# Attention steps of a three-stage kernel: chunk 3 of the scores behind the values, the slot sums behind the reciprocals of head 1, and one copy of x on ScalarE

## The chip, the cores and the metric

The kernel runs on one core of a Trainium2 chip. The metric is the device time of one execution in microseconds; the kernel before was run three times, and its median stands for it. One execution was also profiled, which gives the trace of every engine.

## What is computed

Causal attention over 4 batches, 12 heads, 448 positions and 64 dimensions per head; its output, 1792 tokens of 768, goes through a soft mixture of experts (8 experts with 4 slots each, a softmax over tokens into the slots and one over slots back to the tokens) and then through a feed-forward layer with the activation h cos h.

```python
scores = scale * np.matmul(q, k.transpose(0, 1, 3, 2))      # causal mask, softmax
attn_out = np.matmul(attn, v)                               # per batch and head
x = attn_out.transpose(0, 2, 1, 3).reshape(B * S, H * D)

logits = x @ phi                                            # 1792 x 32
d = softmax(logits, over tokens);  slot_input = d.T @ x
slot_out[e] = np.maximum(slot_input[e] @ w1[e], 0.0) @ w2[e]
x = softmax(logits, over slots) @ slot_out

h = x @ w_in
out = (h * np.cos(h)) @ w_out
```

## The kernel before

Everything is one program for one core, in fp32. The change touches the attention alone, which fills some 225 us of the span; the expert weights stream in behind it, and the feed-forward layer follows.

Heads are handled in pairs: 4 batches with 6 pairs each, 24 pairs in all. Each pair's scores are cut into four chunks of query rows, `qk_mm(p, c)`: chunks 0, 1 and 2 hold 128 queries against 448, 320 and 192 keys, chunk 3 the last 64 queries of both heads against 64 keys. The two heads are j = 0 and 1. Each of the eight PSUM banks is named: banks 0 and 1 take chunk 0 of the two heads, and bank 0 also takes chunk 3 in its last 64 columns (line 281); banks 2 and 3 take chunks 1 and 2. `TA` and `TB` are banks 4 and 5, `OB` bank 6, `MB` bank 7.

For each pair the work goes through these helpers:

- `score` on VectorE adds the mask, takes the row minimum of the negated scores and writes them to SBUF (lines 308 and 311). It returns the exponential on ScalarE (line 313), which also sums the rows.
- `recip` on VectorE inverts the sums of one head (lines 320 and 321), and `norm` on GpSimd scales the exponentials (line 330), four instructions for head 0 (with chunk 3) and three for head 1.
- `t_pair` transposes one half of the normalised scores on TensorE in 64-column blocks into `TA` and `TB` (line 333). `ev_t` copies the two banks to SBUF, one by ScalarE (line 179) and one by VectorE (line 181).
- `pv` multiplies by the values on TensorE into `OB` (line 377), and `ev_o` copies the result by ScalarE into `xts` (line 179), which is x transposed.
- `x_t` transposes x back on TensorE (line 389), head 0 into `OB` and head 1 into bank 1, and `ev_x` copies both into `xk` (line 181), 112 partitions with 256 columns each.

Once per batch comes the part of the experts that needs attention's output: `phi_round` (line 400) gives the logits in `MB`, `be_logits` copies them, `be_rep` (line 409) spreads them, `be_d` takes maximum and exponential, `be_tok` (line 434) and `be_dk` (line 429) transpose them, and `be_u` (line 456) sums x into the slots, one half of a batch's pairs at a time. Its result is added to `uacc` by VectorE (line 460 in the first batch, line 462 later).

The order is written out by hand: `pair_step(t)` issues work of three pairs, `t` (scores), `p1 = t - 1` (normalising and transposing) and `p2 = t - 2` (values and x), and each engine runs its instructions in the order in which they are written there. So an instruction that waits holds up all that stands behind it on its engine. `pair_step` is called for t from 0 to 24; then `tail` closes the last pair and batch. `sc` and `e` call `score` and the exponential that it returned.

Of the kernel before, what the change touches and what calls it, by code (L numbers as in the profile page):

```python
# [15 lines left out]
NB, NH, S, D = 4, 12, 448, 64  # L16
# [140 lines left out]
def moe_stack_kernel(ctx: ExitStack, tc: tile.TileContext, qk, v, cst, phi, w1, w2, w_in, w_out, out):  # L157
    nc = tc.nc

    def pr(key):  # L160
        def deco(fn):
            def run(*a):
                k = key(*a) if callable(key) else key
                if callable(key) and k not in PRI and "." in k:
                    k = k[:k.index(".")]
                o = PRI.get(k, 0)
                if not o:
                    return fn(*a)
                with tc.high_priority(o):
                    return fn(*a)  # L170
            return run
        return deco
# [4 lines left out]
    def copy(e, o, i):  # L177
        if e == "A":
            ACT.activation(o, i, AF.Copy)
        else:  # L180
            ENG[e].tensor_copy(o, i)  # L181
# [85 lines left out]
    def V(p, c, j):  # L267
        c0, n, t = [x for x in VB[p % 2] if x[0] <= c < x[0] + x[1]][0]
        o = 128 * (c - c0) + 64 * j
        return t[:, o:o + 64]  # L270

    def XT(p):
        return xts[:, (p % 4) * 448:(p % 4 + 1) * 448]

    def XK(p):
        i = p % 7
        return xks[i // 4][0:112, (i % 4) * 512:(i % 4 + 1) * 512].rearrange("p (r f) -> p r f", r=4)
# [6 lines left out]
    @pr(lambda p, c: f"qk{c}")  # L284
    def qk_mm(p, c):
        if c == 3:

            for j in range(2):
                PE.matmul(bank[0][64 * j:64 * j + 64, 448:512], lhsT=Q(p)[:, 384 + 64 * j:448 + 64 * j],
                          rhs=K(p)[:, 0:64], start=True, stop=True)  # L290
            return
        q0, ln = CH[c]
        for j in range(2):
            h = slice(64 * j, 64 * j + 64)
            PE.matmul(sreg(j, c), lhsT=Q(p)[h, q0:q0 + 128], rhs=K(p)[h, 0:ln], start=True, stop=True)  # L295

    @pr(lambda p, j, c: f"score{j}{c}")
    def score(p, j, c):
        st_ = pst[p % 2]
        if c == 3:  # L300
            dst, ln, m, col = P0(p), 64, mask0, 3
        else:
            ln = CH[c][1]
            dst, m, col = Pt(p, j)[:, PO[c]:PO[c] + ln], (mask, mask[:, 128:], mask2)[c], 4 * j + c
        sb = sreg(j, c)
        if c == 2:
            blk = lambda x: x.rearrange("p (b f) -> p b f", f=64)
            DVE.tensor_tensor_reduce(out=blk(dst), in0=blk(sb), in1=m, scale=-0.125, scalar=3.0e38,
                                     op0=ALU.add, op1=ALU.min, accum_out=st_[:, col:col + 1])
        else:  # L310
            DVE.tensor_tensor_reduce(out=dst, in0=sb, in1=m, scale=-0.125, scalar=3.0e38,  # L311
                                     op0=ALU.add, op1=ALU.min, accum_out=st_[:, col:col + 1])
        return pr(f"exp{j}{c}")(lambda: ACT.activation(dst, dst, AF.Exp, bias=st_[:, col:col + 1], scale=-1.0,  # L313
                                                       accum_out=st_[:, 8 + col:9 + col]))
# [52 lines left out]
    @pr("pv")  # L367
    def pv(p):
        pt = [pts[:, 1024 * j:1024 * j + 1024] for j in range(2)]
        ops = [(384, 448, 0, [pt[0][:, 384:448], pt[0][:, 960:1024]], True, True),  # L370
               (0, 384, 0, [t[:, 0:384] for t in pt], True, False),
               (64, 384, 1, [t[:, 448:768] for t in pt], False, False),
               (128, 320, 2, [t[:, 768:960] for t in pt], False, False),
               (256, 320, 3, [pt[1][:, 384:448]] * 2, False, True)]
        for a, b, c, r, first, last in ops:
            for j in range(2):
                PE.matmul(OB[64 * j:64 * j + 64, a:b], lhsT=V(p, c, j), rhs=r[j], start=first, stop=last)  # L377

    @pr("evo")
    def ev_o(p):  # L380
        copy(CFG["evo"], XT(p), OB[:, 0:448])
# [3 lines left out]
    @pr("xt")  # L385
    def x_t(p):
        for r in range(4):
            for j, h in enumerate((LO, HI)):
                PE.transpose(XB[j][0:112, 64 * r:64 * r + 64], XT(p)[h, 112 * r:112 * r + 112],
                             cs[h, 64:128] if j else cs[h, 0:64])  # L390

    @pr("evx")
    def ev_x(p, j, e):
        copy(e, XK(p)[:, :, 64 * j:64 * j + 64], XB[j][0:112, 0:256].rearrange("p (r f) -> p r f", r=4))

    @pr("phi")
    def phi_round(b, pr):
        for i in pr:
            r = i % 4
            PE.matmul(MB[32 * r:32 * r + 32, 0:448], lhsT=phs[:, i, :], rhs=XT(b * NPB + i),  # L400
                      start=(i < 4), stop=(i + 4 >= NPB))

    @pr("logits")
    def be_logits(b):
        ACT.activation(ltr, MB[:, 0:448], AF.Copy)
# [26 lines left out]
    def be_tok(b):  # L432
        for r in range(4):
            PE.matmul(MB[0:112, 128 + 32 * r:160 + 32 * r], lhsT=ltr[:, 112 * r:112 * r + 112], rhs=rep[:, 0:32],
                      start=True, stop=True)
        DVE.tensor_copy(ctok[:, 4 * b:4 * b + 4, :], MB[0:112, 128:256].rearrange("p (r s) -> p r s", r=4))
# [14 lines left out]
    def be_u(b, half):  # L451
        ub = TB if (b, half) == (NB - 1, 1) else MB
        for i in range(3):
            p = b * NPB + 3 * half + i
            for r in range(4):
                PE.matmul(ub[32 * r:32 * r + 32, 128 * i:128 * i + 128], lhsT=dk[0:112, r, :], rhs=XK(p)[:, r, :],
                          start=True, stop=True)
        u = uacc[:, 384 * half:384 * half + 384]
        if b == 0:
            DVE.tensor_copy(u, ub[:, 0:384])  # L460
        else:
            DVE.scalar_tensor_tensor(u, u, st[:, 9:10], ub[:, 0:384], op0=ALU.mult, op1=ALU.add)


    def keep_warm(n, t=cs):
        for _ in range(n):
            PE.matmul(bank[3 if t is cs else 7][:, 0:128], lhsT=t[:, 0:128], rhs=t[:, 0:128], start=True, stop=True)
# [14 lines left out]
    def sc(t, j, c):  # L482
        if t < NPAIR:
            ex[j, c] = score(t, j, c)

    def e(t, j, c):
        if t < NPAIR:
            ex[j, c]()

    def pair_step(t):  # L490

        now, prv, pr2 = t < NPAIR, 0 <= t - 1 < NPAIR, 0 <= t - 2 < NPAIR
        bo = {t - NPB * b: b for b in range(NB)}
        p1, p2 = t - 1, t - 2
        if now:
            qk_mm(t, 0)
        if t == 0:
            keep_warm(6, uacc)
        if prv:
            sc(p1, 1, 1)  # L500
            e(p1, 1, 1)
            sc(p1, 1, 2)
            e(p1, 1, 2)
        if 6 in bo:
            phi_round(bo[6], range(4))
        if 8 in bo:
            phi_round(bo[8], range(4, NPB))
            be_logits(bo[8])
        if 9 in bo:
            be_tok(bo[9])  # L510
            be_dk(bo[9])
        sc(t, 0, 0)
        e(t, 0, 0)
        sc(t, 1, 0)
        e(t, 1, 0)
        if now:
            qk_mm(t, 3)
        if pr2:
            pv(p2)
        if 9 in bo:  # L520
            be_u(bo[9], 0)
        if 10 in bo:
            be_u(bo[10], 1)
        if 8 in bo:
            be_rep(bo[8])
        if prv:
            recip(p1, 1)
            for c in range(3):
                norm(p1, 1, c)
        sc(t, 0, 3)  # L530
        if pr2:
            ev_o(p2)
        if prv:
            t_pair(p1, 0)
            ev_t(0, "A")
            ev_t(1, "D")
        e(t, 0, 3)
        if now:
            qk_mm(t, 1)
            qk_mm(t, 2)  # L540
        if 8 in bo:
            be_d(bo[8])
        sc(t, 0, 1)
        e(t, 0, 1)
        sc(t, 0, 2)
        e(t, 0, 2)
        if pr2:
            x_t(p2)
            ev_x(p2, 1, "D")
            ev_x(p2, 0, "D")  # L550
        if prv:
            t_pair(p1, 1)
            ev_t(2, "A")
            ev_t(3, "D")
        if now:
            recip(t, 0)
            for c in range(4):
                norm(t, 0, c)
        if t < NPAIR - 2:
            load_raw(t + 2)  # L560
        if 1 < t < NPAIR:
            load_v(t)
        if t >= 1 and t % 6 != 0 and len(pieces) < NPRE:
            load_piece()
        for _ in range(PL.get(t, 0)):
            load_piece()
# [577 lines left out]
```

## Time and profile before

| what | value |
|---|---|
| median of three runs | 579.81 us (579.77 to 582.02) |
| the profiled execution | 578.87 us, its span 577.1 us |
| TensorE matmul busy, share of the span | 512.5 us, 89% |
| TensorE weight load | 365.2 us, 63% |
| VectorE | 355.1 us, 62% |
| ScalarE | 309.5 us, 54% |
| GpSimd | 184.1 us, 32% |
| DMA moved | 100.36 MB, mean 174 GB/s |
| mean granted TensorE clock | 0.964 of full speed |

The span is from the first to the last instruction; the time of the execution holds some 1.8 us around it. Busy shares are means over stages with different limits: the attention runs to about 225 us, then the expert weights are streamed (to about 300 us), then the feed-forward layer keeps TensorE at 90% and more. Where engines wait is told by the waits and by the timeline of a step, which the prediction goes through.

### The profile page before, as it was taken

What the parts mean: (1) busy time and instruction counts of PE and PEld (TensorE: products, weight loads), DVE (VectorE), ACT (ScalarE), POOL (GpSimd) and SP (SyncE); (2) the same over time, 40 slices, a digit from 0 to 9 for tenths busy, and PEclk for the clock granted to TensorE, in tenths of its full rate; (3) what the DMA queues carried; (4) which work ended last, traced back from release to release, by engine and by line L of the source; (5) the groups of instructions that cost most, each with busy time, mean ns of one, the idle gap of its engine ahead of it and who ended that gap; (6) DMA issues with size and microseconds to landing.
All of it is one profiled execution on the core that took longest, in us unless ns stands there. A gap on an engine that the chain in (4) does not pass through costs nothing.

```text
span 577.1 us, 11159 instructions
## 1 busy us (share of the span) xinstructions
PE 512.5 (89%) x4292; PEld 365.2 (63%) x4292; DVE 355.1 (62%) x897; ACT 309.5 (54%) x711; POOL 184.1 (32%) x251
## 2 busy tenths in 40 slices
PE   6889877887888888988868899999999999999997
PEld 4555545544555556332446687778787777888997
DVE  4575656764774564610148889988798887534532
ACT  3676756764675461101128676665656746543552
POOL 1344424432442340000004352424344246522231
PEclk9798989987997889999999999999999999999999
DMA  5476546573655458999993425332325301202201
GB/s 177 147 250 219 177 142 235 179 247 99 215 165 210 154 213 298 378 422 421 419 367 118 170 82 188 109 110 73 146 84 191 109 1 56 109 1 109 111 1 55
DMA packets 24245, 100.36 MB, mean 174 GB/s; under 512 B 2816, under 2 KB 6912, under 8 KB 18048
## 3 DMA queue, kind: packets, MB, share of 16 engines
q1 hardware_dynamic: 24192, 99.66, 47.8%
q8 instruction: 33, 0.54, 0.4%
q14 instruction: 20, 0.16, 0.1%
HBM read 94.14 MB, written 5.51 MB: 173 GB/s over the span
## 4 chain that ended last, share of the span: by engine, by line
PE 50%; DVE 21%; DMA 15%; ACT 7%; issue 3%; POOL 3%; SPq 0%; DVEq 0%; ACTq 0%; POOLq 0%
PE bank L377 9%; PE bank L879 7%; PE bank L877 7%; PE bank L878 7%; PE bank L295 7%; DMA w<-in_w_dram 6%; DMA zraw<-in_w_out_dram 5%; PE bank L333 5%; DMA zraw<-in_w_in_dram 4%; DVE p L311 3%; POOL p L330 2%; DVE zscr L858 2%; ACT zraw L703 2%; DVE zscr L864 2%; ACT zscr L861 2%
## 5 line engine op out<-in xcount | busy, mean ns | idle before, releaser
L877 PE MATMUL bank<-zg,zhl 128*128 128x512 f32 (+1 forms) x378 | 140.0, 370 | 0.3 <-ACT zhl L725 0.3
L878 PE MATMUL bank<-zg,zhl 128*128 128x512 f32 (+1 forms) x378 | 137.7, 364 | 0.9 <-DVE zhl L738 0.9
L879 PE MATMUL bank<-zg,zhl 128*128 128x512 f32 (+1 forms) x378 | 137.5, 364 | 0.8 <-POOL zg L870 0.8
L870 POOL TENSOR_TENSOR zg<-zscr,zg 128x512 fp32r<-128x512 f32 (+1 forms) x64 | 82.8, 1298 | 140.3 <-ACT zg L867 120.2
L330 POOL TENSOR_SCALAR p<-p,pst 128x448 f32<-128x448 f32 (+3 forms) x168 | 81.3, 502 | 134.8 <-DVE pst L321 94.8
L313 ACT ACTIVATE p<-p,pst 128x448 f32<-128x448 f32 (+3 forms) x168 | 87.5, 521 | 41.6 <-DVE pst L311 41.6
L877 PEld LDWEIGHTS bank<-zg,zhl 128*128 128x128 f32 x378 | 71.5, 189 | 13.7 <-issue 1.4
L878 PEld LDWEIGHTS bank<-zg,zhl 128*128 128x128 f32 x378 | 71.6, 189 | 12.3 <-DVE zhl L738 1.6
L879 PEld LDWEIGHTS bank<-zg,zhl 128*128 128x128 f32 x378 | 71.4, 189 | 12.5 <-POOL zg L870 1.3
L295 PE MATMUL bank<-qk 64*128 64x192 f32 (+2 forms) x288 | 63.0, 466 | 3.5 <-DVE xk L181 3.5
L858 DVE SCALAR_TENSOR_TENSOR zscr<-zscr,bank 128x512 f32<-128x512 int32 (+1 forms) x64 | 38.8, 618 | 32.8 <-ACT zscr L855 32.5
L861 ACT ACTIVATE zscr<-zscr,b_h 128x512 f32<-128x512 f32 (+1 forms) x64 | 42.0, 669 | 31.5 <-DVE zscr L858 31.4
L181 DVE COPY pts<-bank 128x512 f32<-128x512 f32 x48 | 33.0, 687 | 41.8 <-PE bank L333 41.8
L311 DVE CUSTOM_DVE_ANT_0 p<-bank,cs 128x448 f32<-128x448 f32 (+1 forms) x96 | 50.7, 547 | 9.7 <-PE bank L295 9.7
L864 DVE TENSOR_TENSOR zscr<-bank,zscr 128x512 f32<-128x512 f32 (+1 forms) x64 | 39.1, 621 | 18.4 <-ACT zscr L861 18.4
L855 ACT ACTIVATE zscr<-bank,b_q 128x512 int32<-128x512 f32 (+1 forms) x64 | 39.4, 629 | 20.2 <-PE bank L851 20.1
L867 ACT ACTIVATE zg<-zscr 128x512 fp32r<-128x512 f32 (+1 forms) x64 | 36.2, 575 | 26.0 <-DVE zscr L864 25.9
L738 POOL TENSOR_TENSOR zhl<-uacc,zhl 128x768 fp32r<-128x768 f32 (+1 forms) x7 | 10.8, 1550 | 101.6 <-ACT zhl L725 101.6
L703 ACT ACTIVATE zraw<-zraw 128x768 f32<-128x768 f32 x32 | 29.2, 911 | 24.6 <-DMA zraw<-in_w_in_dram 13.2
L333 PE MATMUL bank<-cs,p 64*128 64x64 f32 (+1 forms) x768 | 35.2, 230 | 6.8 <-POOL p L330 6.6
L295 PEld LDWEIGHTS bank<-qk 64*128 64x128 f32 x288 | 29.3, 194 | 14.1 <-DVE xk L181 9.9
L333 PEld LDWEIGHTS bank<-cs,p 64*128 64x128 f32 (+1 forms) x768 | 29.1, 137 | 12.5 <-POOL p L330 10.1
(142 smaller groups left out, 703.7 us busy)
## 6 DMA issues: line engine op xcount, KB each, us to landing
w<-in_w_dram SPq DMA_DIRECT2D x48, 1024.0 KB, 7.9
zraw<-in_w_in_dram SPq DMA_DIRECT2D x16, 768.0 KB, 4.4
zraw<-in_w_out_dram SPq DMA_DIRECT2D x16, 768.0 KB, 4.3
qk<-in_qk_dram SPq DMA_DIRECT2D x24, 480.0 KB, 3.6
xk<-in_v_dram SPq DMA_DIRECT2D x12, 256.0 KB, 3.9
out_dram<-zps SPq DMA_DIRECT2D x8, 256.0 KB, 2.0
xts<-in_v_dram SPq DMA_DIRECT2D x12, 128.0 KB, 3.5
lt<-in_v_dram SPq DMA_DIRECT2D x12, 128.0 KB, 4.1
```

Source lines behind the costliest of these rows:

```text
L295: PE.matmul(sreg(j, c), lhsT=Q(p)[h, q0:q0 + 128], rhs=K(p)[h, 0:ln], start=True, stop=True)
L311: DVE.tensor_tensor_reduce(out=dst, in0=sb, in1=m, scale=-0.125, scalar=3.0e38, op0=ALU.add, op1=ALU.min, accum_out=st_[:, col:col + 1])
L313: return pr(f"exp{j}{c}")(lambda: ACT.activation(dst, dst, AF.Exp, bias=st_[:, col:col + 1], scale=-1.0, accum_out=st_[:, 8 + col:9 + col]))
L330: ENG[CFG["norm"][3 * j + c if c < 3 else 6]].tensor_scalar(dst, dst, st_[:, 24 + col:25 + col], 0.0, op0=ALU.mult, op1=ALU.add)
L333: PE.transpose(out, src, by)
L377: PE.matmul(OB[64 * j:64 * j + 64, a:b], lhsT=V(p, c, j), rhs=r[j], start=first, stop=last)
L861: ACT.activation(y_(s), y_(s), AF.Sin, bias=b_h, scale=1.0)
L864: DVE.tensor_tensor(y_(s), hb[:, 0:n_(s)], y_(s), ALU.mult)
L870: eng.tensor_tensor(g_(s)[1], y_(s), g_(s)[0].bitcast(F32), ALU.subtract)
L877: PE.matmul(o, lhsT=wh, rhs=gh, start=first, stop=False)
L878: PE.matmul(o, lhsT=wl, rhs=gh, start=False, stop=False)
L879: PE.matmul(o, lhsT=wh, rhs=gl, start=False, stop=last)
```

## The change

Three moves inside `pair_step`. The two matmuls of chunk 3 are issued behind `pv` instead of ahead of it. The two calls of `be_u` stand behind `sc(t, 0, 3)` and `ev_o` instead of ahead of `recip(p1, 1)`. `x_t` and the copy of head 1's half of x stand ahead of the exponential of chunk 1, and that copy is made by ScalarE ("A") instead of VectorE ("D"); the copy of head 0's half stays where it was, on VectorE.

```diff
--- before.py
+++ after.py
@@ -513,14 +513,10 @@
         e(t, 0, 0)
         sc(t, 1, 0)
         e(t, 1, 0)
+        if pr2:
+            pv(p2)
         if now:
             qk_mm(t, 3)
-        if pr2:
-            pv(p2)
-        if 9 in bo:
-            be_u(bo[9], 0)
-        if 10 in bo:
-            be_u(bo[10], 1)
         if 8 in bo:
             be_rep(bo[8])
         if prv:
@@ -530,6 +526,10 @@
         sc(t, 0, 3)
         if pr2:
             ev_o(p2)
+        if 9 in bo:
+            be_u(bo[9], 0)
+        if 10 in bo:
+            be_u(bo[10], 1)
         if prv:
             t_pair(p1, 0)
             ev_t(0, "A")
@@ -541,12 +541,13 @@
         if 8 in bo:
             be_d(bo[8])
         sc(t, 0, 1)
+        if pr2:
+            x_t(p2)
+            ev_x(p2, 1, "A")
         e(t, 0, 1)
         sc(t, 0, 2)
         e(t, 0, 2)
         if pr2:
-            x_t(p2)
-            ev_x(p2, 1, "D")
             ev_x(p2, 0, "D")
         if prv:
             t_pair(p1, 1)
```

TensorE, at the start of step 12 (a step with four rounds of `phi_round`). bank_64 is bank 0, bank_65 bank 1, bank_70 `OB`, bank_71 `MB`, bank_68 and bank_69 `TA` and `TB`. Before:

```order
L295 MATMUL bank_64<-qk 128x448
L295 MATMUL bank_65<-qk 128x448
L400 MATMUL bank_71<-xts,phs 32x448 x4
L289 MATMUL bank_64<-qk 64x64 x2
L377 MATMUL bank_70<-pts,xk_77 64x64 x2
L377 MATMUL bank_70<-pts,xk_77 64x384 x2
L377 MATMUL bank_70<-pts,xk_77 64x320 x2
L377 MATMUL bank_70<-pts,xk_77 64x192 x2
L377 MATMUL bank_70<-pts,xk_77 64x64 x2
L333 MATMUL bank_68<-cs,p_74 128x64
```

In the change:

```order
L295 MATMUL bank_64<-qk 128x448
L295 MATMUL bank_65<-qk 128x448
L400 MATMUL bank_71<-xts,phs 32x448 x4
L377 MATMUL bank_70<-pts,xk_77 64x64 x2
L377 MATMUL bank_70<-pts,xk_77 64x384 x2
L377 MATMUL bank_70<-pts,xk_77 64x320 x2
L377 MATMUL bank_70<-pts,xk_77 64x192 x2
L377 MATMUL bank_70<-pts,xk_77 64x64 x2
L289 MATMUL bank_64<-qk 64x64 x2
L333 MATMUL bank_68<-cs,p_74 128x64
```

Chunk 3 (line 289) went from ahead of the ten matmuls of `pv` (two instructions each in the trace) to behind them; the transposes of half 0 (line 333) follow it.

VectorE, in the first step with a `be_u` (step 9); line 460 is its slot sum, lines 320 and 321 are the reciprocals of head 1 and the line 311 behind them is the score of chunk 3:

```order
 L311 ISA p_74,pst_88<-bank_65,cs 128x448
 L311 ISA pst_88 128x1
+L320 TENSOR_SCALAR pst_87<-pst_87 128x3
+L321 RECIPROCAL pst_87<-pst_87 128x3
+L311 ISA p_74,pst_88<-bank_64,qk 128x64
+L311 ISA pst_88 128x1
 L460 COPY uacc<-bank_71 128x384
-L320 TENSOR_SCALAR pst_87<-pst_87 128x3
-L321 RECIPROCAL pst_87<-pst_87 128x3
-L311 ISA p_74,pst_88<-bank_64,qk 128x64
-L311 ISA pst_88 128x1
```

The reciprocals and the score of chunk 3 went ahead of the slot sum.

ScalarE, in an early ordinary step, from the copy of `TA` to the next one. Before:

```order
L179 ACTIVATE pts<-bank_68 128x8x64
L313 ACTIVATE p_73,pst_87<-p_73,pst_87 128x64
L313 ACTIVATE p_73,pst_87<-p_73,pst_87 128x320
L313 ACTIVATE p_73,pst_87<-p_73,pst_87 128x192
L179 ACTIVATE pts<-bank_68 128x8x64
```

In the change:

```order
L179 ACTIVATE pts<-bank_68 128x8x64
L313 ACTIVATE p_73,pst_87<-p_73,pst_87 128x64
L179 ACTIVATE xk_77<-bank_65 112x4x64
L313 ACTIVATE p_73,pst_87<-p_73,pst_87 128x320
L313 ACTIVATE p_73,pst_87<-p_73,pst_87 128x192
L179 ACTIVATE pts<-bank_68 128x8x64
```

The copy of head 1's half of x (out of bank 1) now stands between the exponentials of chunk 3 and of chunk 1.

## Rows read from the trace of the kernel before

**Rows 1.** Busy time by step: window, its length, engines busy us (count), PEclk, DMA share, GB/s.

```profile
29.47:36.73 7.26, 5.85 (x77) 3.88 (x77) 5.11 (x23) 5.43 (x18) 3.38 (x8) 1.00 0.68 238
...
67.37:78.40 11.03, 8.72 (x90) 5.44 (x90) 6.43 (x28) 6.85 (x23) 4.15 (x10) 1.00 0.72 261
...
88.52:96.99 8.47, 6.21 (x100) 4.24 (x101) 5.63 (x24) 5.55 (x18) 3.38 (x8) 1.00 0.63 229
...
131.88:142.71 10.83, 8.49 (x100) 5.50 (x101) 5.64 (x24) 5.39 (x16) 2.62 (x5) 0.78 0.25 79
...
sum 184.80, PE 151.99 PEld 96.39 DVE 114.76 ACT 119.01 POOL 71.08; mean PE 7.24 PEld 4.59 DVE 5.46 ACT 5.67 POOL 3.38
```

**Rows 2.** Who waited for whom, TensorE, 20 to 215: us total, times, longest.

```profile
PE bank L289 <- DVE pst L311: 24.5, 22, 1.9
```

**Rows 3.** Timeline of TensorE in one step: start, us, line, shapes, count, [idle before].

```profile
151.26 0.34 PE L289 MATMUL bank<-qk 128*64 128x64 f32 x4 [1.36 <-DVE pst L311]
151.42 1.47 PE L377 MATMUL bank<-pts,xts 128*64 128x64 f32 x12
...
153.26 0.71 PE L333 MATMUL bank<-cs,p 64*128 64x64 f32 x16
153.81 1.08 PE L295 MATMUL bank<-qk 64*128 64x320 f32 x8
154.73 0.39 PE L389 MATMUL bank<-cs,xts 64*112 64x64 f32 x8
154.95 0.71 PE L333 MATMUL bank<-cs,p 64*128 64x64 f32 x16
155.50 1.61 PE L295 MATMUL bank<-qk 64*128 64x448 f32 x4
157.04 0.96 PE L400 MATMUL bank<-xts,phs 128*32 128x448 f32 x8
158.52 0.34 PE L289 MATMUL bank<-qk 128*64 128x64 f32 x4 [0.52 <-DVE pst L311]
```

**Rows 4.** Timeline of VectorE in the same step.

```profile
151.66 0.17 DVE L320 TENSOR_SCALAR pst<-pst 128x3 f32<-128x3 f32 x1
...
154.04 0.69 DVE L181 COPY pts<-bank 128x512 f32<-128x512 f32 x1 [1.89 <-PE bank L333]
...
155.62 0.75 DVE L181 COPY xk<-bank 112x256 f32<-112x256 f32 x2
...
156.89 0.16 DVE L320 TENSOR_SCALAR pst<-pst 128x4 f32<-128x4 f32 x1
...
157.18 0.46 DVE L311 CUSTOM_DVE_ANT_0 p<-bank,cs 128x320 f32<-128x320 f32 x1
...
157.84 0.62 DVE L311 CUSTOM_DVE_ANT_0 p<-bank,cs 128x448 f32<-128x448 f32 x1
```

**Rows 5.** Timeline of ScalarE in the same step.

```profile
153.38 0.55 ACT L179 ACTIVATE xts<-bank 128x448 f32<-128x448 f32 x1 [0.57 <-PE bank L377]
154.07 0.60 ACT L179 ACTIVATE pts<-bank 128x512 f32<-128x512 f32 x1
154.56 0.34 ACT L313 ACTIVATE p<-p,pst 128x64 f32<-128x64 f32 x1
...
156.02 0.44 ACT L313 ACTIVATE p<-p,pst 128x192 f32<-128x192 f32 x1
...
157.68 0.56 ACT L313 ACTIVATE p<-p,pst 128x320 f32<-128x320 f32 x1 [0.64 <-DVE pst L311]
...
158.68 0.65 ACT L313 ACTIVATE p<-p,pst 128x448 f32<-128x448 f32 x1
```

**Rows 6.** Timeline of GpSimd in the same step.

```profile
152.21 1.54 POOL L330 TENSOR_SCALAR p<-p,pst 128x448 f32<-128x448 f32 x3 [0.18 <-DVE pst L311]
```

**Rows 7.** Timeline of the DMA queue on SP, behind attention.

```profile
226.92 18.15 SPq L254 DMA_DIRECT2D w<-in_w_dram  x12
```

**Rows 8.** The page: GB/s moved in 40 slices of the span.

```profile
GB/s 177 147 250 219 177 142 235 179 247 99 215 165 210 154 213 298 378 422 421 419 367 118 170 82 188 109 110 73 146 84 191 109 1 56 109 1 109 111 1 55
```

## Prediction

> **What bounds the kernel now.** I read the windows by step first, then who waited for whom on TensorE, then one ordinary step engine by engine, and the weight loads last.
>
> The windows give the length of a step, from one chunk 3 to the next [rows 1]. [...] The step that holds `be_d`, `be_tok` and `be_dk` lasts 11.03 (three of these), and the two after it, with `be_u`, some 8.5 each at the full clock (8.47 is shown; six of these). No engine is full in an ordinary step: TensorE 5.85, VectorE 5.11, ScalarE 5.43, GpSimd 3.38 of 7.26. So a loop of waits sets the step, not one engine's work.
>
> The waits name it: the matmuls of chunk 3 (L289) waited 24.5 us for VectorE in 22 steps [rows 2], 1.1 us each. They write bank 0, from which VectorE is still reading the scores of chunk 0, and `pv` stands behind them in TensorE's order. In the ordinary step [rows 3, 4] chunk 3 issues at 151.26, `pv` runs from 151.42 to 153.26, the transposes of half 0 follow, and VectorE, idle for 1.89, gets their bank at 154.04. From there VectorE works nearly without a gap up to the score of chunk 0 at 157.84, and 0.68 later chunk 3 goes, at 158.52. The loop is 2.78 us of TensorE (151.26 to 154.04) and 4.48 of VectorE (154.04 to 158.52): 7.26.
>
> **What the change does to this loop.** *Chunk 3 behind `pv`* (22 steps, no instruction added). `pv` needs the copies of the transposes of half 1, which VectorE has done when it turns to the reciprocal at 156.89, and TensorE, which is through chunk 0 of the next pair by about 157.1 [rows 3, 4]. So `pv` runs under VectorE's scores instead of after them, and chunk 3 finds bank 0 free. Next in TensorE's order stand the transposes of half 0; what they can be late for is GpSimd's scaling.
>
> *One of the two x copies to ScalarE* (23 copies). VectorE loses half of 0.75 [rows 4], 0.37 per step. ScalarE gains a copy of 256 columns per partition, which no row has: its copies of 448 and 512 columns take 0.55 and 0.60 [rows 5], and 0.34 for 64 columns of an exponential is a floor. The line through the two copies gives 0.38, of which 0.27 adds to the engine, since an instruction there starts about 0.1 before the one ahead has ended (154.07 + 0.60 against 154.56). Bounds 0.2 and 0.5. It waits for `x_t` and stands ahead of two exponentials.
>
> *Slot sums behind the reciprocals* (6 steps). VectorE no longer holds the reciprocals of head 1, and with them GpSimd's three scalings, until `be_u` has run on TensorE.
>
> **The new ordinary step, worked out.** Three loops remain.
> - ScalarE. The exponential of chunk 2 (156.02) led to the one of head 1 (157.68) in 1.66: its own end and its sum, a VectorE copy that held the reciprocal back until 156.89, 0.29 to the score at 157.18, and 0.50 to the exponential [rows 4, 5]. That copy comes 0.37 sooner, so the reciprocal waits only for the sum, at about +0.59 instead of +0.87: 1.38. From there ScalarE runs through: 0.56 + 0.44 + 0.65 + 0.65 for four exponentials, 0.44 for the copy of `pv`'s result, 0.49 and 0.33 for the next two, the new 0.27, and 0.56. Sum 1.38 + 4.39 = 5.77.
> - VectorE and GpSimd. From the reciprocal at 156.89 to the score of chunk 0 at 157.84 it is 0.95; two such scores 1.16 at most; from the reciprocals of head 1 (151.66) to the scalings 0.55; three scalings 1.54 [rows 6]; transposes to their copy 0.78; a copy and its release 0.65: 5.63.
> - TensorE's work without waits: 1.84 + 0.17 + 0.54 + 0.92 + 0.22 + 0.55 [rows 3], and about 0.95 for chunk 0 (448 columns, where chunks 1 and 2 stream 512 in 0.92; the 1.61 of its row holds a wait): 5.2.
>
> ScalarE closes last. I take 5.85, for the releases that I have rounded off; bounds 5.6 and 6.5.
>
> **The rest of a batch.** Four rounds of `phi`, 0.96 on TensorE [rows 3], were hidden in the wait for chunk 3; now half of it pushes `x_t` back, for which ScalarE's new copy waits: +0.5. The chain of `be_d`, `be_tok` and `be_dk` added 3.77 to a step (11.03 less 7.26); the change leaves it, and I keep all of it, with 0.3 for `be_rep`, whose cover goes. Each `be_u` added 1.24 (8.5 less 7.26), partly because VectorE waited for it ahead of the reciprocals. Between nothing and all of this I take 0.75, as its 24 small matmuls stay in TensorE's line. That is 0.5 + 3.77 + 0.3 + 1.5 = 6.07 per batch.
>
> **The sum.** Before, at the full clock: 12 x 7.26 + 3 x 11.03 + 6 x 8.5 = 171.2. After: 21 x 5.85 + 3 x 6.07 = 141.1. That is 30.1 less; the first step with `pv` and the last copies give about 1 more: 31.
>
> [...] I let 10 of the 13.6 stay, and 3.5 go.
>
> The saving reaches the end of the kernel. The weight loads that follow are issued when attention has freed its slots (12 of them at 226.92 [rows 7]), so they move with it; and an ordinary step that moved 238 GB/s in 7.26 us [rows 1] asks for 295 in 5.85, well under the 422 that is reached later on [rows 8].
>
> The profiled run took 578.87 (span 577.1 and 1.8 around it): 578.87 - 31 - 3.5 = 544.4. It lies 0.94 under the median of the runs, 579.81, so the forecast is **545 us**. Its own range is 538 to 553: the new copy's bounds are worth -4 and +3 over 23 steps, the chosen `be_u` and 5.85 a few us each way.
>
> **Rivals.**
> *The clock rises altogether (535).* In ordinary steps TensorE had work in 5.85 of 7.26 us; afterwards it has some 5.2 of 5.85 without a wait of over 0.5. If the waits around `be_d` no longer bring the lower level, the other 10 go too: 535. Against it: those steps keep two waits of about 1 us. Chance 0.2. [...]
>
> *ScalarE waits for `x_t` in every step (558).* The new copy stands ahead of the exponentials. In the schedule above `x_t` and ScalarE arrive within 0.1 us of each other, so any lateness of TensorE or of GpSimd's scaling goes straight into the loop. At 0.6 per step: 21 x 0.6 = 12.6, which gives 558. For it: `x_t` in turn reads what ScalarE has copied shortly before. Chance 0.2.
>
> *Nothing to gain (within 0.5%).* If chunk 3's wait only covered another of the same length, the step stays near 7.26. ScalarE's idle stretches (0.57 and 0.64 [rows 5]) would have to come back elsewhere, and I see no instruction that does it. Chance 0.04.
>
> [...] Chance 0.04.
>
> **How the numbers follow.** The forecast has 0.52, the clock 0.2, `x_t` 0.2, the last two 0.04 each. The range takes the first three: from 532 (the clock case with the bounds of the copy) to 562 (the `x_t` case with a dearer copy). About 0.5%, 2.9 us, is what a measurement of this kernel can tell from no change. Faster 0.92, same 0.04, slower 0.04.
>
> **What would show it.** Chunk 3 should hardly wait for VectorE any more (24.5 us before). An ordinary step's window should be 5.7 to 6.0, with ScalarE busy for some 5.6 of it and idle for about 0.4 before the exponential of head 1. In the `be_u` steps the reciprocals of head 1 should come before the slot sums. What is left of the lowered clock should lie around `be_d`. I am wrong if an ordinary step stays above 6.5, or if VectorE's wait for the transposes of half 0 (1.89) is still there.

## The result

The changed kernel takes 531.67 us (median of four runs, 526.26 to 534.57) against 580.91 before, a ratio of 0.912 with a 95% interval of 0.904 to 0.920. (A ratio here is one of mean times over fast runs; the slowest of these four, 534.57 at a mean granted clock of 0.980, counts as a slow one and is left out of it.) Run again beside other experiments it took 527.47 (525.99 to 528.68), ratio 0.910 (0.906 to 0.914). The forecast was 545 with a range of 532 to 562: the direction and the loop of waits were right, the lowered clock was not, and the gain was larger than the range allowed, 49 us where 35 were forecast.

### The profile page after: what moved, and what is told of

Read it like the earlier page. It is cut to its first block, busy times and chain, and to the rows that moved or that the text cites. A ratio compares the mean times of both kernels' runs of the same rounds, so it can differ in the third digit from the quotient of the medians.

```text
span 530.6 us, 11216 instructions
## 1 busy us (share of the span) xinstructions
PE 498.8 (94%) x4292; PEld 364.7 (69%) x4292; DVE 351.2 (66%) x874; ACT 310.5 (59%) x734; POOL 184.3 (35%) x251
## 4 chain that ended last, share of the span: by engine, by line
PE 55%; DVE 17%; DMA 16%; ACT 8%; issue 2%; POOL 1%; SPq 0%; ACTq 0%; POOLq 0%; DVEq 0%
PE bank L377 10%; PE bank L880 7%; PE bank L879 7%; PE bank L878 7%; PE bank L295 7%; DMA w<-in_w_dram 6%; PE bank L333 6%; DMA zraw<-in_w_out_dram 5%; DMA zraw<-in_w_in_dram 4%; DVE zscr L859 2%; ACT zraw L704 2%; DVE zscr L865 2%; ACT zscr L862 2%; PE bank L852 2%; DVE zhl L739 2%
## 5 line engine op out<-in xcount | busy, mean ns | idle before, releaser
L880 PEld LDWEIGHTS bank<-zg,zhl 128*128 128x128 f32 x378 | 71.4, 189 | 12.6 <-POOL zg L871 1.3
L859 DVE SCALAR_TENSOR_TENSOR zscr<-zscr,bank 128x512 f32<-128x512 int32 (+1 forms) x64 | 38.7, 617 | 32.3 <-ACT zscr L856 31.9
L295 PE MATMUL bank<-qk 64*128 64x192 f32 (+2 forms) x288 | 55.6, 462 | 0.6 <-ACT xk L179 0.5
L179 ACT ACTIVATE pts<-bank 128x512 f32<-128x512 f32 x48 | 28.0, 584 | 8.1 <-PE bank L333 7.6
```

The source lines that it names most:

```text
L880: PE.matmul(o, lhsT=wh, rhs=gl, start=False, stop=last)
```

## The profile after

The profiled execution took 532.41 us, its span 530.6. These are the windows by step of the changed kernel, in the columns of [rows 1], in order of time: an ordinary step; the step with four rounds of `phi`, the one after it and the one with the last two rounds and the copy of the logits; the step of `be_d`, `be_tok` and `be_dk` in batch 0; the two `be_u` steps; the step of `be_d` in batch 1; and the 21 steps together.

```profile
26.33:32.04 5.71, 5.69 (x81) 4.23 (x79) 4.95 (x22) 5.36 (x20) 3.38 (x8) 1.00 0.87 306
...
37.77:44.37 6.60, 6.58 (x92) 4.16 (x90) 5.56 (x25) 6.25 (x23) 4.10 (x10) 1.00 0.88 292
44.37:49.68 5.31, 5.31 (x79) 4.02 (x77) 4.32 (x18) 4.70 (x16) 2.67 (x6) 1.00 0.85 297
49.68:56.62 6.94, 6.62 (x89) 4.18 (x86) 5.62 (x25) 6.48 (x24) 4.33 (x10) 1.00 0.56 182
56.62:66.16 9.54, 8.66 (x97) 5.45 (x95) 6.18 (x26) 6.58 (x23) 3.10 (x7) 1.00 0.72 273
66.16:72.25 6.09, 6.09 (x103) 4.51 (x101) 4.87 (x19) 4.67 (x16) 2.74 (x6) 1.00 0.38 115
72.25:78.75 6.50, 6.50 (x105) 4.98 (x103) 5.50 (x23) 5.61 (x20) 3.40 (x8) 1.00 0.83 291
...
97.30:108.29 10.99, 9.85 (x96) 5.98 (x94) 6.25 (x26) 7.58 (x25) 4.36 (x9) 0.89 0.64 245
...
20.56:163.62 143.06, 139.42 (x1820) 96.36 (x1820) 111.42 (x463) 119.80 (x391) 71.29 (x148) 0.98 0.71 245
```

An ordinary step fell from 7.26 to 5.71, and TensorE is now busy for nearly all of it. The 21 steps take 143.06 instead of 184.80. The granted clock, which was 0.75 to 0.83 in seven of them, is below 0.95 in three (0.89, 0.92 and 0.85, in steps of 10.99, 6.53 and 11.17 us).

Who waited for whom on TensorE, over the attention of the changed kernel (us in total, times, longest):

```profile
PE bank L333 <- DVE ctok L436: 2.6, 3, 0.9
PE bank L333 <- POOL p L330: 1.0, 2, 0.7
PE bank L295 <- ACT xk L179: 0.5, 2, 0.3
```

Chunk 3's 24.5 us of [rows 2] are gone altogether: it now follows `pv` without a wait.

```profile
30.25 2.07 PE L377 MATMUL bank<-pts,xk 128*64 128x64 f32 x17
32.05 0.28 PE L289 MATMUL bank<-qk 128*64 128x64 f32 x2
```

What is left in any number is the copy of `be_tok`, once per batch. And ScalarE in an ordinary step:

```profile
28.07 0.57 ACT L179 ACTIVATE pts<-bank 128x512 f32<-128x512 f32 x1
28.55 0.33 ACT L313 ACTIVATE p<-p,pst 128x64 f32<-128x64 f32 x1
...
28.88 0.37 ACT L179 ACTIVATE xk<-bank 112x256 f32<-112x256 f32 x1
29.15 0.55 ACT L313 ACTIVATE p<-p,pst 128x320 f32<-128x320 f32 x1
...
29.69 0.44 ACT L313 ACTIVATE p<-p,pst 128x192 f32<-128x192 f32 x1
...
31.06 0.56 ACT L313 ACTIVATE p<-p,pst 128x320 f32<-128x320 f32 x1 [0.35 <-DVE pst L311]
```

The new copy took 0.37 (0.38 was read off the line through the two longer ones) and moved the next instruction by 0.27 (28.88 to 29.15), as forecast. The way from the exponential of chunk 2 (29.69) to that of head 1 (31.06) is 1.37; the working had 1.38. ScalarE waits only there.

Where the span went, stage by stage, in the stretches of the windows view, before and after: the start 20.53 and 20.56; the 21 steps 184.80 and 143.06; the close of attention 24.13 and 21.00; the stream of expert weights 68.78 and 66.41; the feed-forward layer 278.85 and 279.60. The differences sum to -46.46 (577.09 to 530.63), of which -41.74 fell in the 21 steps and -4.72 outside them.

## The experiments

**One part at a time.** Four kernels ran together; each differs from one of the two kernels in one part. First chunk 3 alone, in the kernel before:

```diff
-        if now:
-            qk_mm(t, 3)
         if pr2:
             pv(p2)
+        if now:
+            qk_mm(t, 3)
```

> Theory (chunk 3's wait was the loop, and the clock follows TensorE's density): an ordinary step falls from 7.26 to about 6.05, set by VectorE and GpSimd with both copies of x (5.63 + 0.37); each be_u still adds its 1.24. At the full clock 147 us for the 21 steps instead of 171; some 9 of the 13.6 us of lowered clock go. 547 us, 543 to 552. Rival 1 (the three moves need each other: with both copies on VectorE, chunk 0 of the next pair waits for bank 1 and holds pv back): ordinary step 6.6, 565 us. Rival 2 (the clock has nothing to do with it): 557 us, with the lowered windows of the kernel before.

Measured: 544.39 us, ratio 0.940 (0.935 to 0.945). The windows of an ordinary step, of the step of `be_d` and `be_dk`, of the first `be_u` step, and of the 21 steps:

```profile
24.72:30.51 5.79, 5.65 (x82) 3.85 (x80) 5.12 (x23) 5.15 (x18) 3.39 (x8) 1.00 0.85 293
...
55.50:67.18 11.68, 10.29 (x98) 6.13 (x95) 6.29 (x25) 6.91 (x23) 3.11 (x7) 0.85 0.57 215
67.18:74.22 7.04, 6.14 (x107) 4.25 (x105) 5.50 (x22) 4.36 (x14) 2.98 (x6) 1.00 0.50 145
18.69:173.15 154.46, 142.71 (x1826) 92.19 (x1823) 115.63 (x484) 115.65 (x369) 71.36 (x148) 0.96 0.66 228
```

This one move gives 36 of the 49 us, what it does to the clock included. The first rival falls: an ordinary step is 5.79, not 6.6. It is even below the 6.05 of the theory, so the loop of VectorE and GpSimd with both copies was put too long by at least a quarter of a microsecond. The second rival (557, the lowered windows of before) falls too: no ordinary step ran at a lowered clock, only the three steps of `be_dk` (0.79 to 0.86) and one behind them (0.90).

Then the change without chunk 3, which stays ahead of `pv`:

```diff
-        if pr2:
-            pv(p2)
         if now:
             qk_mm(t, 3)
+        if pr2:
+            pv(p2)
```

> All of the change but chunk 3. Theory: the old loop stays, shorter by the one copy that VectorE no longer makes: ordinary step 6.9, chunk 3 still waits about 1 us for VectorE; the be_u steps win some 0.5 each. About 10 us at the full clock, the lowered clock stays for the most part: 569 us, 563 to 574. Rival 1 (the copy and the slot sums are worth nothing by themselves): 578 to 581. Rival 2 (the copy is what opened the loop): under 555.

Measured: 562.35 us, ratio 0.972 (0.966 to 0.979), a little below the interval of the theory. An ordinary step is 6.97, and chunk 3 waits as it did:

```profile
28.70:35.67 6.97, 5.38 (x77) 3.75 (x77) 4.83 (x22) 5.72 (x19) 3.40 (x8) 1.00 0.78 251
```

```profile
PE bank L289 <- DVE pst L311: 28.1, 22, 2.0
```

So without chunk 3's move the loop of waits stays and shortens by 0.29, about what VectorE saves on one copy (0.37 was expected); the `be_u` steps win more than the 0.5 expected (7.77 against 8.47). Neither rival came. Eight of the 21 steps still ran at a granted clock below 0.9, three of them ordinary ones (the mean of the 21 is 0.92); with chunk 3's wait gone (the run above) no ordinary step did.

Next the change with `x_t` and both copies where they were, on VectorE:

```diff
-        if pr2:
-            x_t(p2)
-            ev_x(p2, 1, "A")
         e(t, 0, 1)
...
         if pr2:
+            x_t(p2)
+            ev_x(p2, 1, "D")
             ev_x(p2, 0, "D")
```

> The change with x_t and both copies left as they were, on VectorE. Theory: ordinary step 6.05 instead of 5.72, so about 6 to 7 us over the changed kernel: 538 us, 534 to 542; ScalarE no longer closes the loop. Rival (ScalarE's queue is the limit either way and the copy costs there what it saves on VectorE): same as the changed kernel, 531 to 533.

Measured: 538.27 us, ratio 0.929 (0.924 to 0.934), as the theory had it, but not for its reason. An ordinary step is 5.79 against 5.71, not 6.05: there the rival had it right, since ScalarE has no copy to make but takes 1.65 from the exponential of chunk 2 to that of head 1, against 1.37. What the copy on ScalarE saves lies mostly in the step of `be_d` (11.67 here, 9.54 with it), where TensorE waits for VectorE's x copy before chunk 0 of head 1:

```profile
58.00:69.67 11.67, 10.29 (x96) 6.11 (x94) 6.55 (x27) 6.90 (x23) 4.47 (x10) 0.85 0.58 218
```

```profile
PE bank L295 <- DVE xk L181: 3.5, 3, 1.3
```

The two steps did not run at the same clock (0.85 here, 1.00 with the copy). Some 0.6 of the 2.13 is waiting: 1.00 for the x copy, less 0.43 that is saved ahead of `be_tok`'s copy (0.38 against 0.81). The other 1.5 is the lowered clock behind it: `pv` takes 3.31 here, from 66.36 to 69.67, and 1.80 in the changed kernel, from 64.36 to 66.16.

```profile
63.37 1.02 PE L295 MATMUL bank<-qk 64*128 64x448 f32 x2 [1.00 <-DVE xk L181]
...
66.36 2.83 PE L377 MATMUL bank<-pts,xts 128*64 128x64 f32 x12
```

```profile
64.36 1.52 PE L377 MATMUL bank<-pts,xts 128*64 128x64 f32 x12
```

The copy is also worth 0.48 in the step behind each four-round `phi` step (5.79 without it, 5.31 with it) and 0.49 in the first `be_u` step (6.58 against 6.09).

Last of the four, the change with the slot sums ahead of the reciprocals again:

```diff
+        if 9 in bo:
+            be_u(bo[9], 0)
+        if 10 in bo:
+            be_u(bo[10], 1)
         if 8 in bo:
             be_rep(bo[8])
```

(and the same four lines removed behind `ev_o`).

> The change with the slot sums at their old place, ahead of the reciprocals of head 1. Theory: 0.5 to 1.2 us more in each of the six be_u steps, since GpSimd's three scalings and the second transposes come late again: 3 to 7 us over the changed kernel, 535 to 539. Rival (pv and be_u now run so early on TensorE that VectorE no longer waits for the slot sums): same as the changed kernel, 531 to 533.

Measured: 535.60 us, ratio 0.926 (0.922 to 0.930). The two `be_u` steps take 7.05 and 7.04 instead of 6.09 and 6.50, since the transposes of half 1 wait for GpSimd's scalings again, 6.0 us in all against the 1.0 of the changed kernel:

```profile
66.56:73.61 7.05, 6.15 (x107) 4.26 (x105) 5.17 (x21) 5.03 (x17) 2.98 (x6) 1.00 0.48 146
73.61:80.65 7.04, 6.13 (x106) 4.24 (x104) 5.29 (x23) 5.71 (x19) 3.39 (x8) 1.00 0.71 260
```

```profile
PE bank L333 <- POOL p L330: 6.0, 7, 1.0
```

That is 1.5 us per batch, 4.5 in all; the theory stands and the rival falls.

**The clock.** The step of the forecast that failed is the one on the lowered clock, so the next runs asked what lowers it. The fifth kernel is the one before, in its old order, with dummy matmuls in TensorE's waits. They write to `OB` while it is free, and nothing reads them. (The kernel does the like itself at the start and at the close of attention, in `keep_warm`, line 467.)

```diff
+    def fill(n):
+        for _ in range(n):
+            PE.matmul(OB[:, 0:128], lhsT=cs[:, 0:128], rhs=cs[:, 0:128], start=True, stop=True)
...
             be_tok(bo[9])
+            fill(1)
             be_dk(bo[9])
+            fill(3)
+        if 2 < t < NPAIR and 9 not in bo:
+            fill(1 if 6 in bo else 1 if 8 in bo else 4)
         sc(t, 0, 0)
```

> The kernel before, with nothing reordered, and small dummy matmuls on TensorE where it stood idle (four ahead of chunk 3 in an ordinary step, some 1.0 of the 1.36 us; fewer elsewhere). They compute nothing that is used. Theory (TensorE's idle time in attention is what brings the lower clock): steps at the full clock stay at 7.26, and most of the 13.6 us that the lower clock took goes: 570 us, 567 to 573. Rival 1 (the lower clock has another cause, such as where the step of be_d falls): 578 to 582. Rival 2 (the dummies delay chunk 3): an ordinary step above 7.3 at the full clock.

Measured: 567.72 us, ratio 0.979 (0.975 to 0.983). Work was added, nothing was taken away or moved, and the kernel is 13 us faster. An ordinary step is as long as before, with TensorE busy for 6.93 of it instead of 5.85, and none of them is lowered any more; the steps of `be_dk` still are, in all three batches of the stretch (0.88, 0.89 and 0.89):

```profile
20.96:28.21 7.25, 6.93 (x84) 4.83 (x84) 5.11 (x23) 5.42 (x18) 3.37 (x8) 1.00 0.71 244
64.50:76.34 11.84, 10.83 (x99) 7.59 (x99) 6.73 (x28) 7.15 (x23) 4.15 (x10) 0.88 0.68 244
```

There one wait had been left empty, between the two heads of chunk 0:

```profile
71.67 1.02 PE L295 MATMUL bank<-qk 64*128 64x448 f32 x2 [1.01 <-DVE xk L181]
```

A later kernel fills that as well, with four dummies into `MB`:

```diff
+            if c == 0 and j and p in (9, 15, 21):
+                for _ in range(4):
+                    PE.matmul(MB[:, 0:128], lhsT=cs[:, 0:128], rhs=cs[:, 0:128], start=True, stop=True)
             PE.matmul(sreg(j, c), lhsT=Q(p)[h, q0:q0 + 128], rhs=K(p)[h, 0:ln], start=True, stop=True)
```

> The fifth run's kernel (nothing reordered, dummy matmuls in TensorE's waits), with four more dummies in the one long wait that was left empty, between the two heads of chunk 0 in the steps of be_tok (1.0 to 1.26 us, in three steps). In that run each of these steps was still followed by one lowered window. Theory: these go as well, 2 to 3 us: 564 to 566, and the 21 steps take 172. Rival (they come from elsewhere): 567 to 569.

Measured: 565.38 us, ratio 0.978 (0.971 to 0.985). The medians of the two differ by less than their runs scatter, and each is 13 us under the kernel before run beside it (578.43 here); the trace is plain. The lowered clock left these three steps and the ones behind them:

```profile
20.69:29.58 8.89, 8.57 (x84) 5.56 (x85) 5.12 (x23) 5.43 (x18) 3.38 (x8) 0.81 0.59 208
...
65.89:76.94 11.05, 10.72 (x107) 7.36 (x107) 6.44 (x28) 6.86 (x23) 4.16 (x10) 1.00 0.71 244
76.94:85.42 8.48, 7.30 (x109) 5.23 (x109) 5.64 (x24) 5.40 (x16) 2.62 (x5) 1.00 0.43 118
115.68:126.98 11.30, 10.84 (x107) 7.36 (x107) 6.51 (x28) 7.04 (x24) 4.15 (x10) 1.00 0.72 253
20.69:194.22 173.53, 162.39 (x1974) 109.20 (x1975) 114.72 (x484) 118.99 (x369) 71.08 (x148) 0.99 0.61 205
```

It also measures the old order at the full clock: 173.53 less the 1.63 that its one lowered step lost (8.89 against 7.26) is 171.9. The prediction's sum had 171.2.

The kernel before was profiled once more, to see whether its lowered clock is an accident:

> The kernel before once more, for a second profile. Theory: its lowered clock belongs to its waits, so that again some 10 to 16 us of the 21 steps go to it, most in the steps of be_d and be_dk of batches 1 and 2; the steps at the full clock are the same. Rival (the first profile was an accident): under 6 us, and a time near 570.

Measured: 579.96 us (one run). The 21 steps took 185.53 at a mean granted clock of 0.91, 13.6 more than at the full clock. The steps by `be_d` are lowered as before; the two ordinary steps that are lowered are other ones. The sum hardly changed.

```profile
20.95:206.48 185.53, 152.72 (x1819) 96.84 (x1819) 114.79 (x484) 118.99 (x369) 71.08 (x148) 0.91 0.57 191
```

The granted clock in 40 slices of the span (14.4 us each, in tenths), in the first profile and in this one; here the third and the fifth slice are at 8 and the fourth at 9, there it is the other way round:

```profile
PEclk9798989987997889999999999999999999999999
```

```profile
PEclk9889879997998889999989999999999999999999
```

And the changed kernel once more, for the same reason:

> The changed kernel once more, for another profile. If the lowered clock is set by the order of the work, the windows lie in the same steps as before (13 to 14, 20 to 21) and attention ends within 2 us of the other profile; the steps at the full clock are the same to 0.05 us. Rival (they come by chance): other steps, and the median moves by several us, within 526 to 535.

Measured: 527.47 us. Neither answer was right as stated: steps at the full clock agree to 0.03 us, but the windows that were lowered in batches 1 and 2 are not lowered here.

```profile
97.54:107.34 9.80, 8.67 (x97) 5.46 (x95) 6.24 (x26) 6.99 (x24) 3.31 (x7) 1.00 0.74 256
20.84:160.86 140.02, 136.44 (x1820) 94.83 (x1820) 111.32 (x463) 119.49 (x391) 71.12 (x148) 1.00 0.73 250
```

So 140.02 is the changed order at the full clock, and what is left of the lowered clock (3.0 us in the first profile) comes and goes. The distance between the two medians, 531.67 and 527.47, goes with it: the runs without a profile do not show their steps, but each has its mean granted clock, and the eight runs of the changed kernel stand in its order, from 534.57 at 0.980 to 525.99 at 0.997.

**Two tries to go further.** Dummies in the one wait that the changed kernel still has in each batch, between `be_tok` and `be_dk`:

```diff
             be_tok(bo[9])
+            fill(3)
             be_dk(bo[9])
```

> The changed kernel with three dummy matmuls between be_tok and be_dk, where TensorE waited 0.88 us in each batch. Theory: the lowered windows that are left lie right behind this wait, so they go: 3 us at most, 528 to 530. Rival (they are set by more than this wait): same as the changed kernel, 530 to 533.

Measured: 528.54 us, 0.911 (0.906 to 0.916). Its 21 steps took 140.06 at 1.00, but so did the changed kernel's without dummies in the same set of runs (140.02, median 527.47). Inconclusive: there was nothing lowered left for it to show.

```profile
20.46:160.52 140.06, 138.70 (x1838) 96.85 (x1838) 111.33 (x463) 119.52 (x391) 71.11 (x148) 1.00 0.73 253
```

The other moves `be_tok` behind chunk 3, `be_dk` behind the transposes of half 0 and the first `be_u` behind the score of chunk 1:

```diff
-        if 9 in bo:
-            be_tok(bo[9])
-            be_dk(bo[9])
         sc(t, 0, 0)
...
         if 9 in bo:
-            be_u(bo[9], 0)
+            be_tok(bo[9])
...
+        if 9 in bo:
+            be_dk(bo[9])
         if now:
             qk_mm(t, 1)
...
         sc(t, 0, 1)
+        if 9 in bo:
+            be_u(bo[9], 0)
```

> The changed kernel with be_tok behind pv and chunk 3, be_dk behind the transposes of half 0, and the first be_u behind the score of chunk 1, so that TensorE has other work while VectorE copies. Theory (in the step of be_tok the chain of waits is the limit: 9.5 + 6.1 us for two steps against 5.72 + 6.5): two to three us less per batch, 523 to 527. Rival (VectorE's score of chunk 2 now waits for be_u, and this costs as much): 530 to 533.

Measured: 529.54 us, 0.913 (0.909 to 0.917): no gain. The step of `be_tok` got shorter by 1.92 (9.53 to 7.61), the next longer by 2.18 (6.10 to 8.28), as the rival had it, though VectorE's idle time only moved: it now waits for `be_tok`, chunk 1 and `be_u` in the second step, and TensorE has no idle time left there to give.

```profile
56.33:63.94 7.61, 7.54 (x82) 4.22 (x79) 5.04 (x21) 5.62 (x20) 2.43 (x6) 1.00 0.67 224
63.94:72.22 8.28, 8.28 (x114) 6.27 (x114) 6.05 (x25) 5.62 (x20) 3.42 (x8) 1.00 0.62 210
```

## Why the prediction was right and where it was wrong

- *Chunk 3's wait sets the step.* Right. Its 24.5 us went to nothing, an ordinary step to 5.71 (forecast 5.85, with ScalarE's loop at 5.77), and moving chunk 3 alone gives 36 of the 49 us.
- *The sum at the full clock.* Right: 171.2 to 141.1 in the forecast, 171.9 to 140.0 as measured, a gain of 31.9 where 30.1 was worked out. For a batch from 37.77 to 78.75 the working has 6 x 5.85 + 6.07 = 41.2, the trace 40.98; that it is so close is partly luck. The step with four rounds of `phi` costs 0.9 (6.60) and the one behind it, at 5.31, gives 0.4 back: 0.5, as taken. But the working has nothing for the step with the last two rounds and the copy of the logits, 6.94 in batch 0 and some 6.6 later against 5.71. What made up for it: the ordinary step was put 0.14 too long, six times in a batch; the `be_u` steps came out at 6.09 and 6.50, together 1.17 over two ordinary ones where 1.5 was taken; and the step of `be_d` is 9.54 in batch 0 (9.8 later at the full clock) where 9.92 was taken.
- *The copy on ScalarE.* Its duration was right, its use was not where it was put. It was to take 0.37 off the loop of VectorE and GpSimd, which by the working would close last without it (5.63 + 0.37 = 6.0). Without it an ordinary step is longer by only 0.08 (5.79): that loop was put too long, and ScalarE closes the new loop either way (1.66 + 4.39 less the 0.27 of the copy is 5.78). It pays in the steps of `be_d`, where it frees bank 1 in time; in batch 0 the lowered clock behind that wait goes too (11.67 to 9.54).
- *The slot sums.* Right in kind and size: 4.5 us over three batches.
- **The step that failed** is "I let 10 of the 13.6 stay, and 3.5 go". No run shows the 13.6 as such: it is the 184.80 of [rows 1] less the 171.2 of the sum, with 12 ordinary steps, three of `be_d` and six of `be_u`. Of the lowered clock, 12.9 us by the measured full-clock sum (184.80 less 171.9), 3.0 stayed in the first profile (143.06 less 140.02) and none in the second. The profiled run came in 12.0 under the 544.4 that was added up for it, and some 6.4 of that is this term (9.9 went where 3.5 was forecast), 1.8 the sum at the full clock, 3.7 what lies outside the 21 steps. Against letting all of it go stood that "those steps keep two waits of about 1 us". Five of the seven lowered steps of the kernel before do lie in or right behind the step of `be_d` and `be_dk` (the four last windows here and the 10.83 at 0.78 of [rows 1]); the first two are ordinary ones:

```profile
20.53:29.47 8.94, 7.53 (x77) 4.70 (x77) 5.12 (x23) 5.44 (x18) 3.38 (x8) 0.81 0.58 189
...
43.99:52.85 8.86, 8.34 (x85) 4.90 (x85) 5.12 (x23) 5.44 (x18) 3.38 (x8) 0.81 0.54 185
...
78.40:88.52 10.12, 7.84 (x101) 4.97 (x101) 5.63 (x24) 5.40 (x16) 2.62 (x5) 0.83 0.29 83
...
118.78:131.88 13.10, 10.53 (x91) 6.44 (x91) 6.51 (x28) 7.04 (x24) 4.16 (x10) 0.79 0.61 222
...
173.05:185.79 12.74, 10.17 (x91) 6.42 (x91) 6.51 (x28) 7.03 (x24) 4.15 (x10) 0.82 0.67 237
185.79:196.79 11.00, 8.78 (x100) 5.62 (x100) 5.72 (x24) 5.39 (x16) 2.61 (x5) 0.75 0.27 76
```

  But of the waits of about 1 us there only one is left. In that stretch of batch 1 TensorE had waited 1.26 (for VectorE's x copy, ahead of chunk 0 of head 1), 0.38 (for the copy of `be_tok`) and 0.92 (for a score, ahead of chunk 3):

```profile
126.20 1.64 PE L295 MATMUL bank<-qk 64*128 64x448 f32 x2 [1.26 <-DVE xk L181]
...
129.85 1.10 PE L333 MATMUL bank<-cs,dT 128*112 128x128 f32 x4 [0.38 <-DVE ctok L436]
131.88 0.48 PE L289 MATMUL bank<-qk 128*64 128x64 f32 x4 [0.92 <-DVE pst L311]
```

  In the changed kernel the first is 0.26, the second 0.88 and the third gone, and the stretch around them is dense. The copy on ScalarE cut the first and chunk 3's new place ended the third, both parts of the change itself:

```profile
101.93 1.02 PE L295 MATMUL bank<-qk 64*128 64x448 f32 x2 [0.26 <-ACT xk L179]
...
104.73 0.65 PE L333 MATMUL bank<-cs,dT 128*112 128x128 f32 x4 [0.88 <-DVE ctok L436]
```

  That the waits bring the lower clock here is shown by the two kernels with dummies, which changed nothing but what TensorE did in them: the mean granted clock of the 21 steps was 0.97 and 0.99 with the dummies, 0.92 and 0.91 in the two profiles without. The other traces agree. Where the wait of 1.0 to 1.26 ahead of chunk 0 of head 1 stands (the kernel before in both profiles, chunk 3 alone, both copies on VectorE, the first kernel with dummies), the step of `be_dk` or the one behind it was lowered in all 15 cases. Where it is filled or at most 0.26 and chunk 3 no longer waits 0.9 there (the changed kernel in both profiles, with dummies and with `be_tok` later, the slot sums at their old place, the second kernel with dummies), it was in 4 of 18. The rival "the clock rises altogether" was the one that happened, and its chance should have been well over 0.2.
- That rival gave 535, and the time was 531.67 and then 527.47. The range's lower end was to be this case with the bounds of the copy; by the working's own terms that is 535 less 4, 531, where 532 was written. What the rival's sum has too little of lies outside the 21 steps, which gave 4.7 where about 1 was forecast. The close of attention is shorter by 3.1: some 1.4 of it is a lowered stretch at 205 that is gone (a granted clock of 0.69 from 205 to 210.5), and the remainder is `pv` of the last pair, which now stands ahead of the chunk 3 where the stretch begins. The stream of weights took 66.4 instead of 68.8; in its first 10 us the DMA engines moved 418 GB/s instead of 362. With chunk 3 alone and in the second profile of the changed kernel that stage is short too (66.4 and 66.8), without chunk 3's move it is 68.7. Why the DMA engines are fuller there was not tried.
- *Nothing to gain* and a slower time, at 0.04 each, had nothing for them in any run. *ScalarE waits for `x_t` in every step* shows as 1.5 us in eight waits over the whole attention, not 12.6.

## What to carry to other kernels

Look for the small instruction that waits with a long one queued behind it: chunk 3's two matmuls, 0.17 us together, held up the ten of `pv`, 1.84 us together, in 22 steps, and turning the two around gave 36 us, the lowered clock that went with the waits included. When a change takes waits out of TensorE, price the lowered clock with them: add up what the lowered steps cost (here 12.9 us), and look up which waits stand ahead of them and whether the change leaves them: here most of the clock's cost went with the waits (3.0 us were left in one profile, none in the other). A full-clock sum and a clock term are best forecast apart, and the second can be measured cheaply by filling the waits with matmuls that nothing reads.

## What the runs showed of the hardware that was not expected

Dummy matmuls made an unchanged order faster by 13 us (580.97 to 567.72): the stretches at the lowered clock (0.75 to 0.83 in seven steps before, and a mean of 0.97 over the 21 steps with the dummies, 0.92 without) had cost more than filling the waits around them. These waits are short, 1.36 us in an ordinary step of 7.26, and which ordinary steps were lowered differed between two profiles of the same kernel. With dummies in the waits, no ordinary step of the old order was lowered in one kernel and one in the other: the first (20.69 to 29.58, at 0.81), in which `pv` ran low (3.52 us instead of the 1.84 of [rows 3]) before the first dummies came.
